# A chain of attention and two mixture layers on one core: the third token chunk's first expert layer rewritten as seven quarter products per pair of feature tiles

## The chip, the core and the metric

One NeuronCore of a Trainium2 chip runs the whole kernel. The metric is the device time of one execution in microseconds, as the median of several runs. The profile is of one execution, taken by the hardware profiler. The engines are called as the profile calls them: PE (TensorE matmul), PEld (its weight loads), DVE (VectorE), ACT (ScalarE), POOL (GpSimd), SP (SyncE, which issues the large transfers).

## What is computed

The reference, cut to what matters (shapes in comments):

```python
x = attention(q, k, v)               # 2 x 8 heads x 768 x 64, window of 128 and 4 sinks
x = x.transpose(...).reshape(1536, 512)
h = x @ w_in                         # 512 x 2048
y = (maximum(h, 0) + alpha * minimum(h, 0)) @ w_out      # 2048 x 512
p = domain_probs / (domain_probs.sum(-1) + 1e-9)         # 1536 x 4
for e in range(4):
    h = maximum(y @ w1[e], 0)        # 512 x 1024, the first expert layer
    out += p[:, e:e+1] * (h @ w2[e]) # 1024 x 512, the second
```

Everything is float32. The change is in the last loop, for the last 512 of the 1536 tokens.

## The kernel before

**Splits.** Each float32 operand of a matmul is held as two parts of type fp32r, a rounded one (names in h: `wh`, `yh`, `th`) and a rest (`wl`, `yl`, `tl`). A product is three matmuls: high by high, high by low, low by high. ACT makes the high part with a copy, POOL or DVE the low part with a subtraction.

**Tiles.** Tokens stand in three chunks of 512 columns (c = 0, 1, 2). `yh[c]`, `yl[c]` hold the first mixture's output, transposed: 128 partitions by four blocks d of 512 tokens. Feature tiles are 128 wide: tiles 0 to 15 belong to the first mixture, 16 to 47 to the experts. A tile's first weights lie in columns 0 to 511 of `wh[k]`, `wl[k]` and its second weights in columns 512 to 1023.

**Stages.** Attention goes on until about 203 us, with the first mixture's first tiles in between. `rest` then runs the first mixture in blocks of tiles (6 to 10, 11 to 15) over the three chunks, and tiles 16 and 17 over the three chunks; in each of its steps the first layer of one tile runs two steps ahead of the second layer of another. `experts` takes tiles 18 to 47 in 15 pairs (k, k+1), one after another.

**One pair** has three parts on PE, in the order written in the program:
- `four(k)`: the first layer of chunks 0 and 1 for both tiles as one 2 by 2 block product in seven block products instead of eight (Winograd's form). Blocks of the activations are halves of d (two of the four blocks) of chunk 0 or 1, 512 columns wide; the sums S2, S3, S4 of such blocks are in `sh`, `sl`, and S1 takes the place of a block of chunk 1. The blocks of the weights are `b11` to `b22` and their differences T, in `th`, `tl`. One block product is 6 matmuls of 512 columns, so 42 in all. Between products ACT copies the first result (`p1`), DVE adds the others up (`u2`, `u3`, `c22`, `c21`, `c12`), ACT writes the rounded ReLU (`relu_hi`, `hh`) and DVE the rest (`relu_lo`, `hl`). The last two `relu_lo` are put off in `self.later` until `leave()`.
- the first layer of chunk 2 by `s1`, tile by tile: 24 matmuls of 512 columns, then `relu`.
- `out(k, c, hid)` for the three chunks: the second layer, 4 blocks of 6 matmuls of 512 columns for each chunk, 72 in all. After each block DVE adds the result, times the share of the expert, to `acc`.

**Weights of later pairs.** `pair` is a generator of eight steps: four splits (ACT, POOL), the differences T (POOL) and two splits of T. `tick()` lets one step of each open generator be issued, `queue` names those that may begin. `load_due` issues the DMAs that refill the four raw buffers (`raws`). `experts` queues the pair after the next one, and ticks once after chunk 2's first layer and after every second block of `out`.

**Buffers.** `wh` and `wl` come from a ring of six buffers each (`EARLY`) in the pool `work`; tiles 6, 7, 14 and 15 have a place of their own in `late[0]`, `late[1]`, and so have `th`, `tl` of the expert pairs, in turn. The pools `late` and `atk` (attention's split operands) are laid out from the top of the memory downwards (`side="right"`). In this layout the two `late` pools begin at byte 221,152 and 212,960 of a partition, both 32 past a multiple of 64; every other tile that PE reads as weights after attention begins at a multiple of 64. PSUM has eight banks, two of each tag (`h`, `o`) in each of two pools (`psum[0]`, `psum[1]`). `out` uses the two `o` banks of `psum[1]`, chunk 2's first layer those of `psum[0]`.

Of the kernel before, what the change touches and what calls it, by code (L numbers as in the profile page):

```python
# [21 lines left out]
P = 128  # L22
# [31 lines left out]
class Body:  # L54
    def __init__(self, ctx, tc, a):
        self.tc, self.nc, self.a = tc, tc.nc, a
        self.base = ctx.enter_context(tc.tile_pool(name="base", bufs=1))
        self.wraw, self.wh, self.wl = {}, {}, {}

        self.raws = [self.base.tile([P, 2 * CH], F32, name=f"wraw{i}") for i in range(RAW)]  # L60
        self.qks = [self.base.tile([P, KW + UN], F32, name=f"qk{i}") for i in range(QK)]
# [227 lines left out]
    def relu_hi(self, h, name):  # L289
        hh = self.wide.tile([P, CH], F32R, tag="gh", name=f"hh{name}", bufs=6)  # L290
        hl = self.wide.tile([P, CH], F32R, tag="gl", name=f"hl{name}", bufs=6)
        self.nc.scalar.activation(hh, h, AF.Relu)
        return hh, hl

    def relu_lo(self, h, parts):
        hh, hl = parts
        self.nc.vector.scalar_tensor_tensor(hl, h, 0.0, hh.bitcast(F32), ALU.max, ALU.subtract)

    def relu(self, h, name):
        parts = self.relu_hi(h, name)  # L300
# [6 lines left out]
    def sums(self):  # L307

        nc, (a, b) = self.nc, (self.acc[0], self.acc[1])

        def split(i, d, x, eng):
            hi, lo = self.sh[i][:, d, :], self.sl[i][:, d, :]
# [4 lines left out]
        t, u = [self.raws[2 + d][:, CH:] for d in range(2)]  # L317
        for d in range(2):
            nc.vector.tensor_tensor(one[d], b[:, d, :], b[:, 2 + d, :], ALU.add)
            nc.vector.tensor_tensor(t, one[d], a[:, d, :], ALU.subtract)  # L320
            split(2, d, t, nc.gpsimd)
            yield
            nc.vector.tensor_tensor(u, a[:, 2 + d, :], t, ALU.subtract)
            split(4, d, u, nc.gpsimd)
            yield
            nc.vector.tensor_tensor(t, a[:, d, :], b[:, d, :], ALU.subtract)
            split(3, d, t, nc.gpsimd)
            yield

        self.sh[1], self.sl[1] = self.xh[1][:, :2, :], self.xl[1][:, :2, :]  # L330
        for d in range(2):
            split(1, d, one[d], nc.vector)
        yield

    def four(self, k):

        nc, mm = self.nc, self.nc.tensor.matmul
        while any(j <= 2 * k for j in self.queue + [j for j, _ in self.flight]):
            self.load_due()
            self.tick()  # L340
        xh, xl, (w, v) = self.xh, self.xl, (k, k + 1)
        low, high = slice(0, UN), slice(UN, CH)
        B = {11: (w, low), 21: (w, high), 12: (v, low), 22: (v, high)}
        B = {i: (self.wh[x][:, c], self.wl[x][:, c]) for i, (x, c) in B.items()}
        T = [(self.th[k][:, i * UN:(i + 1) * UN], self.tl[k][:, i * UN:(i + 1) * UN]) for i in range(4)]
        A = {11: (xh[0][:, :2, :], xl[0][:, :2, :]), 12: (xh[0][:, 2:, :], xl[0][:, 2:, :]),
             22: (xh[1][:, 2:, :], xl[1][:, 2:, :])}
        S = {i: (self.sh[i], self.sl[i]) for i in range(1, 5)}
# [9 lines left out]
        p = [self.psum[i // 2].tile([P, CH], F32, tag="h", name=f"h{k}_{i}", bufs=2) for i in range(4)]  # L358
        p1, u2, u3, c22 = [self.raws[i][:, CH:] for i in range(4)]
        c21, c12 = [self.qks[2 + i][:, :CH] for i in range(2)]  # L360

# [3 lines left out]
        product(p[0], A[11], B[11], True)  # L365
# [7 lines left out]
        h22 = self.relu_hi(c22, f"{k}_22")  # L373
        product(p[0], A[12], B[21], False)
        h11 = self.relu_hi(p[0], f"{k}_11")
        self.relu_lo(c22, h22)
        self.relu_lo(p[0], h11)
        product(p[2], A[22], T[3], False)
        add(c21, p[2], u2)
        h21 = self.relu_hi(c21, f"{k}_21")  # L380
        product(p[3], S[4], B[22], False)
        add(c12, p[3], u2)
        h12 = self.relu_hi(c12, f"{k}_12")
        self.later = [lambda: self.relu_lo(c21, h21), lambda: self.relu_lo(c12, h12)]
        self.hid[k] = [(h11, h12), (h21, h22)]

    def out(self, k, c, hid):

        nc, mm, e = self.nc, self.nc.tensor.matmul, (k - N1) * P // F2
        for d in range(CH // P):  # L390
            ps = self.psum[1].tile([P, CH], F32, tag="o", name=f"o{k}_{c}_{d}", bufs=2)
# [9 lines left out]
            if d % 2:  # L401
                self.load_due()
                self.tick()
# [7 lines left out]
    def experts(self):  # L411
        for k in range(PAIR1, NW, 2):
            if k > PAIR1:
                self.four(k)
            if k + 4 < NW:
                self.queue.append(2 * (k + 4))
            last = []
            for x in range(2):
                ps = self.psum[0].tile([P, CH], F32, tag="o", name=f"h{k}_c{x}", bufs=2)
                self.s1(k + x, self.xh[2], self.xl[2], ps)  # L420
                self.leave()
                last.append(self.relu(ps, f"{k}_c{x}"))
            self.load_due()
            self.tick()
            for c, hid in enumerate(self.hid[k] + [last]):
# [243 lines left out]
    def ahead(self):  # L669
# [6 lines left out]
        self.sh, self.sl, self.th, self.tl, self.hid, self.later = {}, {}, {}, {}, {}, []  # L676
# [113 lines left out]
    def rest(self, pool, units, blk0):  # L790
# [10 lines left out]
        for i in (2, 3, 4):  # L801
            self.sh[i] = pool.tile([P, 2, CH], F32R, name=f"s{i}h")
            self.sl[i] = pool.tile([P, 2, CH], F32R, name=f"s{i}l")
        sums = self.sums()
        with tc.tile_pool(name="psc", bufs=1, space=PSUM) as psc:
            psum = self.psum = [self.psb, psc]
            gs, outs = {}, None
            for i in range(len(steps) + 2):
# [34 lines left out]
                while PAIR1 <= nxt < PAIR1 + 4 and last[nxt + 1 - SLOTS] <= i:  # L843
# [21 lines left out]
                if (k, c) in [(n1 - 1, 2), (n1, 0)]:  # L865
# [151 lines left out]
```

## Time and profile before

| | us |
|---|---|
| median of 3 runs | 906.77 |
| lowest, highest | 905.07, 911.1 |
| profiled execution | 906.78 |
| its span, first to last instruction | 905.0 |

The profiled execution's time is 1.8 us over its span. A busy row of PE counts matmuls that overlap in the pipeline, so distances between starts are read instead. In a timeline row the columns are the start, the duration, the engine, the line, the operation, what it writes from what it reads, the shape, and in brackets the idle time before it with what ended it.

### The profile page before, as it was taken

How to read it: one execution, taken by the hardware profiler on the slowest of the kernel's cores; microseconds unless marked ns; L12 is line 12 of the kernel's file. 1: busy time of each engine (PE TensorE's matmuls, PEld its weight loads, DVE VectorE, ACT ScalarE, POOL GpSimd, SP SyncE). 2: the span in 40 equal slices, each digit the busy share in tenths (PEclk: the TensorE clock that was granted, in tenths of full speed). 3: DMA queues.
4: the chain of work that ended last, by engine and by line, in shares of the span. 5: the costliest groups of instructions: out<-in, count | busy, mean ns of one | idle time of the engine just before them, and what ended most of it. 6: DMA issues, size and time to landing. Idle time of an engine off the chain costs nothing.

```text
span 905.0 us, 12418 instructions
## 1 busy us (share of the span) xinstructions
PE 891.7 (99%) x4670; PEld 739.1 (82%) x4670; DVE 530.0 (59%) x999; ACT 317.2 (35%) x719; POOL 365.0 (40%) x346
## 2 busy tenths in 40 slices
PE   8999999998999999999999999999999999999997
PEld 5678999998888888888888888888888888888886
DVE  6778877648994543545545555455555545555554
ACT  4787766754431222332222231232123113212210
POOL 2456654525672454675415422440442244034000
PEclk9999999999999999999999999999999999999999
DMA  6554432202331020001011101100110111010003
GB/s 184 173 198 145 142 116 93 78 1 95 116 117 47 24 70 1 1 24 47 23 48 47 47 0 47 47 29 18 47 47 1 47 47 38 10 47 1 1 1 144
DMA packets 23718, 54.47 MB, mean 60 GB/s; under 512 B 3168, under 2 KB 3168, under 8 KB 23648
## 3 DMA queue, kind: packets, MB, share of 16 engines
q1 hardware_dynamic: 23504, 53.57, 18.0%
q8 instruction: 39, 0.64, 0.3%
q14 instruction: 31, 0.25, 0.1%
q10 hardware_dynamic: 144, 0.00, 0.0%
HBM read 50.42 MB, written 3.15 MB: 59 GB/s over the span
## 4 chain that ended last, share of the span: by engine, by line
PE 92%; DVE 4%; ACT 1%; issue 1%; POOL 0%; DVEq 0%; ACTq 0%; POOLq 0%
PE o L397 9%; PE o L396 9%; PE o L395 9%; PE h L354 5%; PE h L356 5%; PE h L355 5%; PE h L250 5%; PE h L251 5%; PE h L252 5%; PE o L259 5%; PE o L260 5%; PE o L261 4%; PE h_c L250 3%; PE pv L640 3%; PE h_c L251 3%; PE h_c L252 3%
## 5 line engine op out<-in xcount | busy, mean ns | idle before, releaser
L400 DVE SCALAR_TENSOR_TENSOR acc<-o,prob,acc 128x512 f32<-128x512 f32 x180 | 135.2, 751 | 100.5 <-PE o L397 100.5
L136 POOL TENSOR_TENSOR wl<-wraw,wh 128x512 fp32r<-128x512 f32 x60 | 77.2, 1298 | 273.4 <-ACT wh L135 273.4
L395 PE MATMUL o<-wh,hh 128*128 128x512 f32 x240 | 93.4, 389 | 0.0
L396 PE MATMUL o<-wl,hh 128*128 128x512 f32 x240 | 93.4, 389 | 0.0
L397 PE MATMUL o<-wh,hl 128*128 128x512 f32 x240 | 93.4, 389 | 0.0
L250 PE MATMUL h<-xh,wh 128*128 128x256 f32 (+1 forms) x264 | 90.2, 342 | 0.0
L252 PE MATMUL h<-xh,wl 128*128 128x256 f32 (+1 forms) x264 | 87.7, 332 | 0.0
L251 PE MATMUL h<-xl,wh 128*128 128x256 f32 (+1 forms) x264 | 87.6, 332 | 0.0
L286 POOL TENSOR_TENSOR gl<-qk,gh 128x512 fp32r<-128x512 f32 (+1 forms) x36 | 48.8, 1356 | 72.1 <-ACT gh L285 69.9
L285 ACT ACTIVATE gh<-qk 128x512 fp32r<-128x512 f32 (+1 forms) x36 | 21.5, 598 | 123.9 <-DVE qk L284 121.2
L366 ACT ACTIVATE wraw<-h 128x512 f32<-128x512 f32 x15 | 9.0, 598 | 156.8 <-PE h L356 156.8
L363 DVE TENSOR_TENSOR wraw<-h,wraw 128x512 f32<-128x512 f32 x45 | 31.1, 692 | 51.0 <-PE h L356 49.4
L283 DVE TENSOR_SCALAR qk<-h,alpha 128x512 f32<-128x512 f32 (+1 forms) x36 | 25.3, 704 | 54.6 <-PE h L252 54.5
L260 PE MATMUL o<-gl,wh 128*128 128x512 f32 (+1 forms) x144 | 54.0, 375 | 1.9 <-POOL gl L286 1.9
L250 PEld LDWEIGHTS h<-xh,wh 128*128 128x128 f32 x264 | 49.9, 189 | 6.6 <-issue 1.7
L259 PE MATMUL o<-gh,wh 128*128 128x512 f32 (+1 forms) x144 | 53.8, 374 | 0.5 <-ACT gh L285 0.5
L252 PEld LDWEIGHTS h<-xh,wl 128*128 128x128 f32 x264 | 49.9, 189 | 5.0
L251 PEld LDWEIGHTS h<-xl,wh 128*128 128x128 f32 x264 | 50.0, 189 | 4.9
L261 PE MATMUL o<-gh,wl 128*128 128x512 f32 (+1 forms) x144 | 53.7, 373 | 0.0
L572 ACT ACTIVATE p<-p,nmax 128x288 f32<-128x288 f32 (+1 forms) x96 | 47.8, 500 | 15.9 <-DVE nmax L551 15.8
L396 PEld LDWEIGHTS o<-wl,hh 128*128 128x128 f32 x240 | 45.0, 188 | 9.4
L395 PEld LDWEIGHTS o<-wh,hh 128*128 128x128 f32 x240 | 45.0, 188 | 9.4
(172 smaller groups left out, 2295.8 us busy)
## 6 DMA issues: line engine op xcount, KB each, us to landing
wraw<-in_w SPq DMA_DIRECT2D x32, 512.0 KB, 3.7
wraw<-in_w SPq DMA_DIRECT2D x64, 256.0 KB, 2.9
qk<-in_qk SPq DMA_DIRECT2D x21, 352.0 KB, 3.0
v<-in_v SPq DMA_DIRECT2D x12, 256.0 KB, 3.4
out<-acc SPq DMA_DIRECT2D x12, 256.0 KB, 2.3
qk<-in_qk SPq DMA_DIRECT2D x8, 272.0 KB, 3.2
qk<-in_qk SPq DMA_DIRECT2D x11, 176.0 KB, 3.0
qk<-in_qk SPq DMA_DIRECT2D x8, 136.0 KB, 3.5
```

The costliest lines, as they stand in the source:

```text
L136: nc.gpsimd.tensor_tensor(lo, x, hi.bitcast(F32), ALU.subtract)
L250: mm(ps, wh[:, c], xh[:, dk, :], start=dk == 0, stop=False)
L251: mm(ps, wh[:, c], xl[:, dk, :], start=False, stop=False)
L252: mm(ps, wl[:, c], xh[:, dk, :], start=False, stop=dk == DM // P - 1)
L259: mm(outs[dt], wh[:, c], gh, start=first and begins[dt], stop=False, skip_group_check=True)
L260: mm(outs[dt], wh[:, c], gl, start=False, stop=False, skip_group_check=True)
L261: mm(outs[dt], wl[:, c], gh, start=False, stop=last, skip_group_check=True)
L286: nc.gpsimd.tensor_tensor(gl, g, gh.bitcast(F32), ALU.subtract)
L395: mm(ps, hh[:, n], wh, start=x == 0, stop=False)
L396: mm(ps, hh[:, n], wl, start=False, stop=False)
L397: mm(ps, hl[:, n], wh, start=False, stop=x == 1)
L400: nc.vector.scalar_tensor_tensor(acc, ps, self.prob[:, nt, e:e + 1], acc, ALU.mult, ALU.add)
```

## The change

- `products` is the body of `four`, now with the operands, PSUM tiles, temporaries and results as arguments. `four` calls it as before for chunks 0 and 1.
- `halves(k)` calls it for chunk 2, whose 512 tokens are taken as two halves of 256: seven block products of 6 matmuls of 256 columns, 42 in all. It uses one `o` bank for each of its four PSUM tiles, and 256-column pieces of `qks[:2]`, `warm` and `masks[1]` as temporaries.
- `sums` goes on for three more steps that make S1 to S4 of chunk 2. S2, S3 and S4 lie in `late[0]`, `late[1]`, S1 in the place of a block of chunk 2. `rest` calls it in three more places.
- `th`, `tl` come from the ring `work` like `wh`, `wl`: three of its six buffers for a pair.
- `experts` queues only the next pair, and `out` issues loads and a tick after each block. `out` takes the `o` banks of both PSUM pools in turn. `leave()` is called in `products` after its second product, and after `halves`.
- A tile of 32 bytes a partition is placed at the top, before the `atk` and `late` pools, which lie 32 bytes lower.

```diff
+        top = ctx.enter_context(tc.tile_pool(name="top", bufs=1, side="right"))
+        self.pad = top.tile([P, 8], F32, name="pad")
...
-        late = self.late[k // 2 % 2]
-        th = self.th[k] = late.tile([P, 2 * CH], F32R, tag="wh", name=f"th{k}", bufs=1)
-        tl = self.tl[k] = late.tile([P, 2 * CH], F32R, tag="wl", name=f"tl{k}", bufs=1)
+        th = self.th[k] = self.work.tile([P, 2 * CH], F32R, tag="wh", name=f"th{k}", bufs=EARLY)
+        tl = self.tl[k] = self.work.tile([P, 2 * CH], F32R, tag="wl", name=f"tl{k}", bufs=EARLY)
...
+        a11, a12, a21, a22 = [y[:, d:d + 2, n:n + UN] for n in (0, UN) for d in (0, 2)]
+        late = [[pool.tile([P, 4, UN], F32R, tag=tag, name=f"s2_{tag}", bufs=1) for tag in ("wh", "wl")]
+                for pool in self.late[:2]]
+        self.s2 = {2 + i: [x[:, i % 2 * 2:i % 2 * 2 + 2, :] for x in late[i // 2]] for i in range(3)}
+        self.s2[1] = [x[2][:, :2, UN:] for x in (self.xh, self.xl)]
+        one, t, u = [x.rearrange("p (d n) -> p d n", d=2) for x in (self.qks[0][:, :CH], t, u)]
+        nc.vector.tensor_tensor(one, a21, a22, ALU.add)
+        sub(t, one, a11)
+        split(self.s2[2], t, nc.gpsimd)
+        yield
+        sub(u, a12, t)
+        split(self.s2[4], u, nc.gpsimd)
+        sub(t, a11, a21)
+        split(self.s2[3], t, nc.gpsimd)
+        yield
+        split(self.s2[1], one, nc.vector)
+        yield
...
         product(p[1], S[2], T[1], True)
+        self.leave()
         add(u2, p[1], p1)
...
+    def halves(self, k):
+        xs = (self.xh, self.xl)
+        A = [[x[2][:, d:d + 2, n:n + UN] for x in xs] for n, d in ((0, 0), (0, 2), (UN, 2))]
+        p = [self.psum[i].tile([P, CH], F32, tag="o", name=f"c{k}_{j}", bufs=2)[:, :UN]
+             for j, i in enumerate((0, 1, 0, 1))]
+        temps = [x[:, n:n + UN] for x in self.qks[:2] for n in (0, UN)] + [self.warm, self.masks[1]]
+        h = [self.hidden(f"{k}_c{i}") for i in range(2)]
+        parts = [[x[:, n:n + UN] for x in h[f]] for n in (0, UN) for f in range(2)]
+        self.products(k, A, self.s2, p, temps, parts)
+        self.hid.append(h)
...
-            ps = self.psum[1].tile([P, CH], F32, tag="o", name=f"o{k}_{c}_{d}", bufs=2)
+            ps = self.psum[(d + 1) % 2].tile([P, CH], F32, tag="o", name=f"o{k}_{c}_{d}", bufs=2)
...
-            if d % 2:
-                self.load_due()
-                self.tick()
+            self.load_due()
+            self.tick()
...
-            if k + 4 < NW:
-                self.queue.append(2 * (k + 4))
-            last = []
-            for x in range(2):
-                ps = self.psum[0].tile([P, CH], F32, tag="o", name=f"h{k}_c{x}", bufs=2)
-                self.s1(k + x, self.xh[2], self.xl[2], ps)
-                self.leave()
-                last.append(self.relu(ps, f"{k}_c{x}"))
+            if k + 2 < NW:
+                self.queue.append(2 * (k + 2))
+            self.halves(k)
+            self.leave()
...
-                while PAIR1 <= nxt < PAIR1 + 4 and last[nxt + 1 - SLOTS] <= i:
+                if nxt == PAIR1 and last[nxt + 1 - SLOTS] <= i:
...
-                if (k, c) in [(n1 - 1, 2), (n1, 0)]:
+                if (k, c) in [(n1 - 1, 2), (n1, 0), (n1, 1)] or (k, c, f) == (n1, 2, N1):
                     next(sums)
```

## Rows read from the trace of the kernel before

**Rows 1.** The page: busy time of the engines, and PE's granted clock in slices.

```profile
PE 891.7 (99%) x4670; PEld 739.1 (82%) x4670; DVE 530.0 (59%) x999; ACT 317.2 (35%) x719; POOL 365.0 (40%) x346
PEclk9999999999999999999999999999999999999999
```

**Rows 2.** The page: the chain that ended last, shares of the span by engine.

```profile
PE 92%; DVE 4%; ACT 1%; issue 1%; POOL 0%; DVEq 0%; ACTq 0%; POOLq 0%
```

**Rows 3.** PE's waits: who was waited for, total us, times, longest.

```profile
PE h_c L250 <- DVE acc L863: 0.2, 1, 0.2
```

**Rows 4.** Timeline of PE, one pair: where its three parts and the next pair begin.

```profile
647.39 0.39 PE L354 MATMUL h<-yh,wh 128*128 128x512 f32 x1
...
657.13 0.39 PE L250 MATMUL h_c<-yh,wh 128*128 128x512 f32 x1
...
662.58 0.39 PE L395 MATMUL o<-wh,hh 128*128 128x512 f32 x1
...
678.90 0.39 PE L354 MATMUL h<-yh,wh 128*128 128x512 f32 x1
```

**Rows 5.** Timeline of PE in the same pair: two matmuls three apart on `tl`.

```profile
652.02 0.39 PE L356 MATMUL h<-yh,tl 128*128 128x512 f32 x1
...
652.72 0.40 PE L356 MATMUL h<-yh,tl 128*128 128x512 f32 x1
```

**Rows 6.** Timeline of PE at the end of attention: two runs of 256-column matmuls.

```profile
201.74 0.28 PE L250 MATMUL h<-xh,wh 128*128 128x256 f32 x1
...
203.06 0.28 PE L252 MATMUL h<-xh,wl 128*128 128x256 f32 x1
...
205.33 0.28 PE L259 MATMUL o<-gha,wh 128*128 128x256 f32 x1
...
207.84 0.28 PE L250 MATMUL h<-xh,wh 128*128 128x256 f32 x1
```

**Rows 7.** Timeline of PE in the block of tiles 6 to 10: starts of four steps.

```profile
247.94 0.39 PE L259 MATMUL o<-gh,wh 128*128 128x512 f32 x1
...
250.67 0.39 PE L250 MATMUL h<-xh,wh 128*128 128x512 f32 x1
...
253.46 0.39 PE L259 MATMUL o<-gh,wh 128*128 128x512 f32 x1
...
256.19 0.39 PE L250 MATMUL h<-xh,wh 128*128 128x512 f32 x1
```

**Rows 8.** Timeline of all engines around the end of `four`, same pair.

```profile
649.92 0.40 PE L356 MATMUL h<-s2h,tl 128*128 128x512 f32 x1
650.43 0.69 DVE L363 TENSOR_TENSOR wraw<-h,wraw 128x512 f32<-128x512 f32 x1 [2.09 <-PE h L356]
...
657.33 0.69 DVE L363 TENSOR_TENSOR qk<-h,wraw 128x512 f32<-128x512 f32 x1 [0.70 <-PE h L356]
...
657.94 1.47 DVE L297 SCALAR_TENSOR_TENSOR hl<-qk,hh 128x512 fp32r<-128x512 f32 x2
658.06 0.63 ACT L292 ACTIVATE hh<-qk 128x512 fp32r<-128x512 f32 x1 [0.76 <-DVE qk L363]
```

**Rows 9.** Groups of DVE and ACT by shape: count, then busy us, mean ns.

```profile
L284 DVE SCALAR_TENSOR_TENSOR qk<-h,qk 128x256 f32<-128x256 f32 x6 | 2.5, 424 | 0.2
L320 DVE TENSOR_TENSOR wraw<-wraw,acc 128x512 f32<-128x512 f32 x2 | 2.7, 1351 | 0.1
L326 DVE TENSOR_TENSOR wraw<-acc,acc 128x512 f32<-128x512 f32 x2 | 1.4, 698 | 0.0
L285 ACT ACTIVATE gh<-qk 128x256 fp32r<-128x256 f32 x6 | 2.5, 418 | 12.1 <-DVE qk L284 9.4 <-PE h L252 2.7
```

**Rows 10.** Timeline of POOL: the end of one stretch of `pair` work, and the next stretch.

```profile
641.71 1.29 POOL L136 TENSOR_TENSOR tl<-t,th 128x512 fp32r<-128x512 f32 x1
664.03 1.30 POOL L136 TENSOR_TENSOR wl<-wraw,wh 128x512 fp32r<-128x512 f32 x1 [21.02 <-ACT wh L135]
...
673.18 1.29 POOL L136 TENSOR_TENSOR tl<-t,th 128x512 fp32r<-128x512 f32 x1
```

More of the change, by code (lines that the diff above doesn't have):

```diff
@@ L307, in sums, with sub, split @@
     def sums(self):
-        nc, (a, b) = self.nc, (self.acc[0], self.acc[1])
-        def split(i, d, x, eng):
-            hi, lo = self.sh[i][:, d, :], self.sl[i][:, d, :]
+        nc, (a, b, y) = self.nc, [self.acc[c] for c in range(NC)]
+        def sub(out, a, b):
+            nc.vector.tensor_tensor(out, a, b, ALU.subtract)
+        def split(to, x, eng):
+            hi, lo = to
             nc.scalar.activation(hi, x, AF.Copy)
@@ L317, in sums @@
         t, u = [self.raws[2 + d][:, CH:] for d in range(2)]
+        s = [{i: [x[:, d, :] for x in self.s01[i]] for i in (2, 3, 4)} for d in range(2)]
         for d in range(2):
             nc.vector.tensor_tensor(one[d], b[:, d, :], b[:, 2 + d, :], ALU.add)
[L320 to L321 removed]
+            sub(t, one[d], a[:, d, :])
+            split(s[d][2], t, nc.gpsimd)
             yield
[L323 removed]
@@ L331, in sums @@
         for d in range(2):
-            split(1, d, one[d], nc.vector)
+            split([x[:, d, :] for x in self.s01[1]], one[d], nc.vector)
         yield
-    def four(self, k):
-        nc, mm = self.nc, self.nc.tensor.matmul
-        while any(j <= 2 * k for j in self.queue + [j for j, _ in self.flight]):
-            self.load_due()
-            self.tick()
[L341 to L344, printed above, removed]
+        a11, a12, a21, a22 = [y[:, d:d + 2, n:n + UN] for n in (0, UN) for d in (0, 2)]
@@ L348, in four @@
-        S = {i: (self.sh[i], self.sl[i]) for i in range(1, 5)}
+        b11, b21, b12, b22 = B
+        a11, a12, a22 = A
+        h11, h12, h21, h22 = hid
+        p1, u2, u3, c22, c21, c12 = temps
         def product(ps, a, b, first):
@@ L356, in product @@
                 mm(ps, bl[:, c], ah[:, d, :], start=False, stop=d == 1, skip_group_check=True)
-        p = [self.psum[i // 2].tile([P, CH], F32, tag="h", name=f"h{k}_{i}", bufs=2) for i in range(4)]
-        p1, u2, u3, c22 = [self.raws[i][:, CH:] for i in range(4)]
-        c21, c12 = [self.qks[2 + i][:, :CH] for i in range(2)]
         def add(out, a, b):
             nc.vector.tensor_tensor(out, a, b, ALU.add)
-        product(p[0], A[11], B[11], True)
+        product(p[0], a11, b11, True)
         nc.scalar.activation(p1, p[0], AF.Copy)
         product(p[1], S[2], T[1], True)
+        self.leave()
         add(u2, p[1], p1)
@@ L372, in four @@
         add(c22, p[3], u3)
-        h22 = self.relu_hi(c22, f"{k}_22")
-        product(p[0], A[12], B[21], False)
-        h11 = self.relu_hi(p[0], f"{k}_11")
+        self.relu_hi(c22, h22)
+        product(p[0], a12, b21, False)
+        self.relu_hi(p[0], h11)
         self.relu_lo(c22, h22)
         self.relu_lo(p[0], h11)
-        product(p[2], A[22], T[3], False)
+        product(p[2], a22, T[3], False)
         add(c21, p[2], u2)
-        h21 = self.relu_hi(c21, f"{k}_21")
-        product(p[3], S[4], B[22], False)
+        self.relu_hi(c21, h21)
+        product(p[3], S[4], b22, False)
         add(c12, p[3], u2)
-        h12 = self.relu_hi(c12, f"{k}_12")
+        self.relu_hi(c12, h12)
         self.later = [lambda: self.relu_lo(c21, h21), lambda: self.relu_lo(c12, h12)]
-        self.hid[k] = [(h11, h12), (h21, h22)]
+    def four(self, k):
+        while any(j <= 2 * k for j in self.queue + [j for j, _ in self.flight]):
+            self.load_due()
+            self.tick()
+        xs = (self.xh, self.xl)
+        A = [[x[c][:, d:d + 2, :] for x in xs] for c, d in ((0, 0), (0, 2), (1, 2))]
+        p = [self.psum[i // 2].tile([P, CH], F32, tag="h", name=f"h{k}_{i}", bufs=2) for i in range(4)]
+        temps = [x[:, CH:] for x in self.raws] + [x[:, :CH] for x in self.qks[2:4]]
+        h = [self.hidden(f"{k}_{i}") for i in range(4)]
+        self.products(k, A, self.s01, p, temps, h)
+        self.hid = [h[:2], h[2:]]
+    def halves(self, k):
+        xs = (self.xh, self.xl)
+        A = [[x[2][:, d:d + 2, n:n + UN] for x in xs] for n, d in ((0, 0), (0, 2), (UN, 2))]
[6 more added lines that the diff above has]
+        self.hid.append(h)
     def out(self, k, c, hid):
@@ L801, in rest @@
         for i in (2, 3, 4):
-            self.sh[i] = pool.tile([P, 2, CH], F32R, name=f"s{i}h")
-            self.sl[i] = pool.tile([P, 2, CH], F32R, name=f"s{i}l")
+            self.s01[i] = [pool.tile([P, 2, CH], F32R, name=f"s{i}{x}") for x in "hl"]
         sums = self.sums()
```

36 lines of the change are left out of this document (18 added, 18 removed).

## The prediction

> **What bounds the kernel now.** I read the page first: PE is busy for 99% of the span and its granted clock is at the upper of its two levels, 2.4 GHz, in all 40 slices [rows 1]. The chain of waits says the same from the end backwards: 92% of it is PE [rows 2]. PE's waits show that in the whole expert stage it waited once, 0.2 us, at the first chunk 2 matmul of pair 18 [rows 3]. So from 236 us on nothing but the number of matmuls and the distance from one start to the next sets the time, and only distances are worth reading; all other engines matter only where they could make PE wait. The timeline of one pair gives the distances [rows 4]: `four` takes 657.13 - 647.39 = 9.74 us for 42 matmuls (0.232 each), chunk 2's first layer 662.58 - 657.13 = 5.45 us for 24 (0.227 each), `out` 678.90 - 662.58 = 16.32 us for 72 (0.2267 each), the pair 31.51 us. The other pairs repeat this within 0.01 us, 15 pairs in all.
>
> **The same matmul has two paces.** 512 columns at 2.4 GHz are 213.3 ns; 226.7 is 13.3 more, and 232 is 19 more. The slow pace is that of `four`: two matmuls three apart on `tl` start 0.70 us apart, 0.233 each [rows 5]. What sets it apart is the weight operand: `th`, `tl` lie in the `late` pools, 32 bytes past a multiple of 64, all other weights of this stage at a multiple. The block of tiles 6 to 10 shows it again [rows 7]: the steps that begin at 247.94 and 253.46 are on tiles 8 and 9 and take 2.73 us for 12 matmuls; the one between, 253.46 - 250.67 = 2.79 us, is on tile 6, which lies in `late`. I take the address as the cause; that the `late` pools are also the topmost memory is a rival below.
>
> **Part 1, chunk 2 in quarter products.** Removed on PE: 24 matmuls of 512 columns, 5.44 us a pair. Added: 42 of 256. Their pace is read at the end of attention, where PE runs 256-column matmuls without a break [rows 6]: 1.32 us for 11 distances and 2.51 for 21, so 0.120 both times, again 13.3 ns over the columns (106.7 ns). 42 x 0.120 = 5.04 us. Gain 0.40 us a pair, x 15 = 6.1 us. The ends: the rounding of the rows allows 0.119 to 0.121; the operands of S2 to S4 and the PSUM order are new here, so I widen that to 0.117 and 0.123, a gain of 8.0 or 4.2 us. Equality is at 5.44 / 42 = 0.1296.
> The Trainium skill speaks against this part: TensorE: Matmul & The Clock Gate, "Back-to-back issue gap", gives a sustained spacing, set by matmul and weight load together, of about 81 ns at 128 columns and 131 ns at 512; read in between, an estimate of 98 ns at 256, 42 would cost 4.1 us where 24 cost 3.1, a loss of 15 us in all. The trace doesn't agree: 227 ns at 512 and 120 at 256 [rows 4, 6], and I go by the rows.
>
> **Part 2, T in the ring.** All weights of `four` are then at a multiple of 64, and 42 x 0.2267 = 9.52 us replace 9.74: 0.22 us a pair, 3.3 us in all. The 9.74 is taken whole: it has the products on `wh` in it that stand between those on `th` and are slowed along with them.
>
> **Part 3, the 32-byte tile.** It moves the `late` pools to a multiple of 64. Four tiles (6, 7, 14, 15) are used in three chunks and two layers: 24 steps, each 2.79 - 2.72 = 0.07 us too long, with 0.01 in the step ahead of it [rows 7]: 24 x 0.08 = 1.9 us. Attention's operands move too; they are some 116 matmuls of 288 columns at most, so between nothing and 116 x 6.5 ns = 0.75 us; I take nothing, as no row shows a slow pace at that shape.
>
> **What lies beside PE.** Per pair, DVE gets five adds of 256 columns (0.42 each [rows 9]) and four short ReLU rests for two long ones, 2.4 us more of 31; ACT one copy and four short for two long. What matters is the order in `halves`, with T the start of its first product (657.13 here) and 0.72 us for each product. DVE still has `four`'s last add from T + 0.20 and the two deferred `relu_lo`, which end at T + 2.28 [rows 8]; `leave()` puts them ahead of the first add of `halves`, so they are what the adds queue behind. ACT's last `hh` ends at T + 1.56, `p1` with 0.42 [rows 9] at T + 2.0. Then u2 ends at T + 2.70, u3 at T + 3.12 (its product is there at 17 x 0.12 + 0.51 = T + 2.55, the 0.51 being the lag from the last matmul's start to DVE's [rows 8]), c22 at T + 3.69. PE's sixth product, which needs u3 to have read its bank, starts at T + 3.60, the seventh, behind c22, at T + 4.32. Margins 0.48 and 0.63: no wait, so this costs nothing, but if DVE were half a microsecond later it would. `out` then begins on the bank that u2 has read and has four banks instead of two, so no wait there.
> `pair` work is now done in one go between `halves` and the next `four`. POOL's share of a pair is ten operations, 10.4 us from 664.03 to 674.47 [rows 10]; it can begin about T + 6.9 as now and ends near T + 17.5, while the next `four` needs `th` at its second product, T + 5.04 + 16.32 + 1.36 = T + 22.7. The ring holds: the pair's three buffers of each kind were released with the pair before the last. The loads of one pair's raw tiles are issued during the pair before, on SP, which has nothing else until the last pair's stores; taken as nothing, and 5 us of room cover them.
> The three more steps of `sums` run once, beside the block of tiles 16 and 17: four DVE operations between 0.70 and 1.35 us [rows 9], three splits. They can hold up the first `four` by one such operation at most, between 0 and 1.35 us, once; I take 0, as DVE is busy for 59% of the span [rows 1]. The 0.2 us wait of [rows 3] stays.
>
> **Sum.** 6.1 + 3.3 + 1.9 = 11.3 us off the span of 905.0, which gives 893.7. The profiled execution took 906.78, 1.8 over its span and equal to the median of 906.77; so I forecast 895.4 us, 1.2% less. With the ends above (pace 0.117 to 0.123, attention, `sums`) 893 to 898.
>
> **Rivals.**
> - *A short hand-back wait in `halves`.* The margins of 0.48 and 0.63 are read from a chain of six operations; a lag of 0.1 more at each step of the chain would use them up. A wait of 0.3 us a pair (two thirds of the smaller margin) costs 4.5 us: 899.9. Against it: the same chain in `four` doesn't stop PE once.
> - *The `late` pools are slow because of where they are, not because of the 32 bytes.* Then part 3 gives nothing (1.9 us lost), and 18 of the 42 quarter products' matmuls, which read S2 to S4 from there as the moving operand, could lose the same 6.5 ns: 18 x 6.5 x 15 = 1.8 us. 899.1. For it: before, place and address go together in every slow row, so no row can tell them apart; that the address has the larger part is a judgement.
> - *Half the columns are not half the time.* If what a matmul costs beyond its columns doubled in products with short operands (13.3 to 26.6 ns), 42 x 0.133 = 5.60 us: part 1 loses 0.15 us a pair, 8.3 us behind forecast: 903.7. Against it: the 32 distances of [rows 6].
> - *Slower: DVE and POOL hold each other up at the start of `halves`.* The rows have the same subtraction at 698 and at 1351 ns [rows 9]. If the two deferred `relu_lo`, with two operands in SBUF each, took 1.35 instead of 0.69, u3 would end at T + 4.35 instead of 3.12 and PE would wait 0.75 us, with 0.2 for starting again 0.95 a pair: 14.2 us, 909.6. It decides from a wait of 0.75 us a pair. The Trainium skill has this rule: SBUF — State Buffer, "Who interferes with whom", where a DVE operation with two SBUF inputs and a POOL operation lock each other out; the 1351 ns agree. Against it: it needs POOL at work from T to T + 2.3, and POOL is idle from 643.0 to 664.03, before and after T [rows 10]; the change doesn't bring its next work forward.
> - *That the change is faster than counted:* if short matmuls ran near the bare 106.7 ns, 42 x 13.3 ns x 15 = 8.4 us more: 887.0. No row shows it.
>
> **How the numbers follow.** Forecast 0.68; short wait 0.11; place of the pools 0.10; width 0.04; slower 0.05; much faster 0.02. The likeliest case gives the time, 895.4. The range 892.5 to 901.5 holds the forecast with its ends and the first two rivals, and leaves out the others and their tails, under 2 in 10. A measurement of this kernel can tell about 1% from no change, 897.7 on the one side and 915.8 on the other. Faster by over 1%: the forecast but for its upper tail, the last case, and the weak ends of the first two, 0.70. Within 1%: 0.27, the slower rival's 909.6 with it. Slower by over 1%: 0.03, for that rival with a longer wait.
>
> **What the changed profile would show.** Right: a pair of 30.88 us between the first L-lines of `products`; 42 matmuls of 512 columns in 9.52, 42 of 256 in 5.04, `out` unchanged at 16.32; steps on tiles 6, 7, 14 and 15 at 2.72; no PE wait inside `halves` in the list of waits. Wrong: a distance over 0.25 us at the sixth or seventh quarter product, with DVE as releaser (first rival or, with `relu_lo` at over 1 us, the slower one); steps on tile 6 still at 2.79 and quarter products with S2 to S4 slower than those without (second); an even 0.13 over all 42 (third); PE waiting for POOL at the second product of `four` would mean that `pair` isn't done in time, which I have ruled out by 5 us.

## The result, and the profile after

The changed kernel took 898.83 us (median of four runs, 894.62 to 899.06), the kernel before beside it 906.73 (905.07 to 911.1): a ratio of 0.9889, with an interval of 0.9857 to 0.9922. That is 1.1% faster, inside the range of 892.5 to 901.5, and 3.4 us over the forecast of 895.4. The profiled execution took 898.79 us, its span 897.0, again 1.8 less.

Here "after" is the changed kernel; its lines are L373 to L375 for the products, L435 to L437 for `out`, L298 for `relu_lo`, L378 for the adds, L381 for `p1`, and the results of chunk 2's quarter products are called `c`. The page of after: busy times, PE's clock in slices, and the chain's shares by engine.

```profile
PE 884.5 (99%) x4940; PEld 749.2 (84%) x4940; DVE 561.7 (63%) x1109; ACT 328.9 (37%) x768; POOL 368.9 (41%) x349
PEclk9699999999999999999999999999999999999999
PE 94%; DVE 3%; ACT 1%; issue 1%; POOL 0%; DVEq 0%; ACTq 0%; POOLq 0%
```

Two things differ from [rows 1, 2]: 270 more matmuls (15 pairs by 42 - 24), and a 6 in the second slice of the clock, where before had 9. The first is the change; the second is taken up below.

PE's timeline of the pair that answers to [rows 4]: the starts of `four`, of the quarter products, of `out` and of the next `four`, and between them the first matmul of each quarter product.

```profile
645.17 0.39 PE L373 MATMUL h<-yh,wh 128*128 128x512 f32 x1
...
654.69 0.28 PE L373 MATMUL c<-yh,wh 128*128 128x256 f32 x1
...
655.40 0.29 PE L373 MATMUL c<-s_wh,th 128*128 128x256 f32 x1
...
656.10 0.28 PE L373 MATMUL c<-s_wh,th 128*128 128x256 f32 x1
...
656.78 0.28 PE L373 MATMUL c<-yh,th 128*128 128x256 f32 x1
...
657.49 0.28 PE L373 MATMUL c<-yh,wh 128*128 128x256 f32 x1
...
658.20 0.28 PE L373 MATMUL c<-yh,th 128*128 128x256 f32 x1
...
658.92 0.29 PE L373 MATMUL c<-s_wh,wh 128*128 128x256 f32 x1
...
659.62 0.39 PE L435 MATMUL o<-wh,hgh 128*128 128x512 f32 x1
...
675.95 0.39 PE L373 MATMUL h<-yh,wh 128*128 128x512 f32 x1
```

`four` takes 654.69 - 645.17 = 9.52 us (forecast 9.52), the quarter products 4.93 (5.04), `out` 16.33 (16.32); the pair 30.78 (30.88, and 31.51 before). The quarter products don't all run at one pace. The third, on S3 (`s_wh` is the buffer that holds its high part), takes 656.78 - 656.10 = 0.68 us, 0.113 a matmul; the first six-matmul stretch, on `yh`, and the sixth take 0.71 to 0.72, 0.118 to 0.120. From the first `four` to the last matmul of the span it is 478.3 us before and 467.4 after: 10.9 us less.

DVE, ACT and POOL beside it (start, duration; "x3" is three in a row; in brackets idle time and who ended it). They answer to [rows 8, 10].

```profile
654.89 0.69 DVE L378 TENSOR_TENSOR qk<-h,wraw 128x512 f32<-128x512 f32 x1 [0.67 <-PE h L375]
655.50 1.48 DVE L298 SCALAR_TENSOR_TENSOR hgl<-qk,hgh 128x512 fp32r<-128x512 f32 x2
656.89 1.47 DVE L378 TENSOR_TENSOR qk<-c,qk 128x256 f32<-128x256 f32 x3
...
656.15 0.36 ACT L381 ACTIVATE qk<-c 128x256 f32<-128x256 f32 x1
...
638.53 2.53 POOL L139 TENSOR_TENSOR tl<-t,th 128x512 fp32r<-128x512 f32 x2
661.38 2.57 POOL L139 TENSOR_TENSOR wl<-wraw,wh 128x512 fp32r<-128x512 f32 x2 [20.32 <-ACT wh L138]
...
669.32 2.54 POOL L139 TENSOR_TENSOR tl<-t,th 128x512 fp32r<-128x512 f32 x2
```

With T = 654.69, the two deferred `relu_lo` run from T + 0.81 to T + 2.29 (forecast: to T + 2.28), the three adds end at T + 3.67 (forecast for c22: 3.69), POOL idles for 20.32 us across T and ends the next pair's work at T + 17.2 (17.5). PE's waits (who was waited for, total us, times, longest):

```profile
PE o L262 <- POOL gl L288: 2.5, 3, 0.9
...
PE s L568 <- DVE nmax L586: 1.0, 1, 1.0
...
PE c L373 <- DVE acc L897: 0.2, 1, 0.2
```

There is none inside the quarter products; the 0.2 us of [rows 3] stayed.

So the expert stage gave more than forecast, and yet the kernel is later than forecast. The difference arises before the expert stage: the first `four` starts at 423.79 us, 2.9 us later than before (420.90), though part 3 should have brought it forward. The table of windows (busy time by engine, then the granted clock, 1.00 for 2.4 GHz and 0.50 for 1.2) shows where. After:

```profile
20.00:25.00 5.00, 3.94 (x14) 2.21 (x15) 2.89 (x12) 3.34 (x11) 2.22 (x2) 0.66 0.53 162
25.00:30.00 5.00, 5.00 (x18) 2.82 (x15) 3.47 (x12) 0.42 (x1) 1.72 (x3) 0.50 0.76 228
30.00:35.00 5.00, 5.00 (x16) 2.78 (x16) 1.31 (x5) 2.84 (x10) 1.44 (x2) 0.50 0.68 210
35.00:40.00 5.00, 5.00 (x24) 3.28 (x20) 3.25 (x11) 2.20 (x7) 0.73 (x1) 0.63 0.36 127
```

The same stretch before:

```profile
20.00:25.00 5.00, 3.79 (x15) 1.89 (x15) 3.65 (x14) 2.97 (x10) 1.55 (x3) 0.82 0.48 155
25.00:30.00 5.00, 4.63 (x24) 2.93 (x21) 3.62 (x13) 1.58 (x6) 2.22 (x3) 0.84 0.84 255
30.00:35.00 5.00, 4.50 (x27) 2.60 (x26) 3.54 (x15) 3.51 (x14) 2.44 (x3) 1.00 0.95 267
```

A mean of 0.66 over 5 us is (1 - 0.66) / 0.5 x 5 = 3.4 us at the lower level. Summed up, after ran 3.4 + 5 + 5 + 3.7 = 17.1 us of attention at 1.2 GHz, before 1.8 + 1.6 = 3.4. PE did the same ahead of it in both: it waited 1.0 us for the DVE operation that makes `nmax` out of earlier scores (the wait on `nmax` above; PE's timelines of after, then of before):

```profile
21.62 1.65 PE L568 MATMUL s<-qk 64*128 64x128 f32 x4 [1.00 <-DVE nmax L586]
```

```profile
22.37 1.16 PE L533 MATMUL s<-qk 64*128 64x128 f32 x4 [1.00 <-DVE nmax L551]
```

The theory that I took to the chip: the pair became 0.72 us shorter for the reasons forecast, the weights' address sets the pace of part 2 and 3, and the length of the low-clock stretch has nothing to do with the change. The rivals: the topmost place sets the pace (the prediction's second rival); quarter products gain only because the moving operand or some address is good, not by their columns; the change itself prolongs the low stretch.

### The profile page after: what moved, and what is told of

It reads as the page before. It is cut to its first block, busy times and chain, and to the rows that moved or that the text cites. A ratio compares the mean times of both kernels' runs of the same rounds, so it can differ in the third digit from the quotient of the medians.

```text
span 897.0 us, 13164 instructions
## 1 busy us (share of the span) xinstructions
PE 884.5 (99%) x4940; PEld 749.2 (84%) x4940; DVE 561.7 (63%) x1109; ACT 328.9 (37%) x768; POOL 368.9 (41%) x349
## 4 chain that ended last, share of the span: by engine, by line
PE 94%; DVE 3%; ACT 1%; issue 1%; POOL 0%; DVEq 0%; ACTq 0%; POOLq 0%
PE o L436 9%; PE o L437 9%; PE o L435 9%; PE h L373 5%; PE h L375 5%; PE h L252 5%; PE h L374 5%; PE h L253 5%; PE h L254 5%; PE o L261 5%; PE o L262 5%; PE o L263 5%; PE pv L675 3%; PE c L373 3%; PE c L375 3%; PE c L374 3%
## 5 line engine op out<-in xcount | busy, mean ns | idle before, releaser
L436 PE MATMUL o<-wl,hgh 128*128 128x512 f32 x240 | 93.6, 390 | 0.0
L437 PE MATMUL o<-wh,hgl 128*128 128x512 f32 x240 | 93.5, 390 | 0.0
L435 PE MATMUL o<-wh,hgh 128*128 128x512 f32 x240 | 93.5, 390 | 0.0
L252 PE MATMUL h<-xh,wh 128*128 128x256 f32 (+1 forms) x264 | 90.2, 342 | 0.0
L378 DVE TENSOR_TENSOR wraw<-h,wraw 128x512 f32<-128x512 f32 x45 | 31.1, 692 | 48.2 <-PE h L375 46.3
L381 ACT ACTIVATE wraw<-h 128x512 f32<-128x512 f32 x15 | 8.9, 596 | 140.9 <-PE h L375 140.9
L252 PEld LDWEIGHTS h<-xh,wh 128*128 128x128 f32 x264 | 50.0, 189 | 6.5 <-issue 1.7
L437 PEld LDWEIGHTS o<-wh,hgl 128*128 128x128 f32 x240 | 45.1, 188 | 9.4
L435 PEld LDWEIGHTS o<-wh,hgh 128*128 128x128 f32 x240 | 45.1, 188 | 8.8
```

Source lines behind the costliest of these rows:

```text
L252: mm(ps, wh[:, c], xh[:, dk, :], start=dk == 0, stop=False)
L435: mm(ps, hh[:, n], wh, start=x == 0, stop=False)
L436: mm(ps, hh[:, n], wl, start=False, stop=False)
L437: mm(ps, hl[:, n], wh, start=False, stop=x == 1)
```

## The experiments

A name with a_ is an edit of the changed kernel, one with b_ an edit of the kernel before. Times are medians; the ratio is to the kernel before, run beside it. The granted clock is that of the whole span, and it tells the length of the low stretch: 0.997 or more for at most a few us of it, about 0.99 for a long one (13.7 us in the profiled a_again and a_yshift, 17.1 in after, b_pad32, a_pad96 and a_mixed). Since either can occur in one and the same kernel, the runs of before fall into two groups, 905.0 to 907.1 and 910.7 to 911.8 us, and so do those of after, 892.9 to 895.4 and 898.7 to 899.5; medians are compared only at like clock.

### The tile's size: address or place?

Five runs put the `late` pools at other addresses. Before without a tile has them at 224 past a multiple of 256, and the change at 192.

```diff
+        top = ctx.enter_context(tc.tile_pool(name="top", bufs=1, side="right"))
+        self.pad = top.tile([P, 8], F32, name="pad")     # b_pad32: before with the tile
+        self.pad = top.tile([P, 16], F32, name="pad")    # b_pad64: before, 64 bytes
-        self.pad = top.tile([P, 8], F32, name="pad")     # a_nopad: after without the tile
+        self.pad = top.tile([P, 24], F32, name="pad")    # a_pad96: after, 96 bytes
+        self.pad = top.tile([P, 56], F32, name="pad")    # a_pad224: after, 224 bytes
```

a_pad224 also has the two fillers (idle matmuls) of a_before, told further down, and is compared with a_before. The expectations, in the order of the diff:

> The kernel before with the 32-byte tile alone. If the address sets the pace of the late weights: th products and steps on tiles 6, 7, 14, 15 go from 0.233 us a matmul to the 0.229 that the changed kernel shows on tile 6, so four takes 9.6 us for 9.74 and a step on tile 6 2.75 for 2.79, some 3 us in all off 906.8. If the place at the top of the memory sets it: 0.233 and 2.79 stay, 906.8. The stretch of low clock near 22 us after the start may be short or long in either.

> The kernel before with a tile of 64 bytes: the late pools move further down than with 32, but their address is again 32 past a multiple of 64. Address: 0.233 us a matmul on th and 2.79 us a step on tile 6, as before. Place: whatever 32 bytes lower gave, 64 gives too.

> The changed kernel without the 32-byte tile. Forecast's part 3: steps on tile 6 back at 2.79 us, 1 to 2 us more in all. The quarter products whose moving operand S2 to S4 lies in late run at 0.113 us in the changed kernel, those on yh at 0.120. If that comes from where late lies: 0.113 again, 4.93 us for 42. If from its address: another pace, 0.120 or over, 5.04 us or more.

> The changed kernel with a tile of 96 bytes: the late pools begin at a multiple of 128. If the weights' price goes by the distance from a multiple of 128: steps on tile 6 at 2.72 us instead of 2.75. If the moving operand is fast because it starts 64 past a multiple of 128 while the weights start at a multiple: S2 to S4 products slow down from 0.113 to 0.120, 42 in 5.04 us. If it is the place: 0.113 stays, 4.93.

> The kernel a_before with the late pools at 0 modulo 256 instead of 192 (a tile of 224 bytes instead of 32). Address: steps on tile 6 fall from 2.747 to 2.72 us, the rest of part 3, 0.6 us in all; the quarter products on S2 to S4 rise from 0.113 to about 0.120, 42 in 5.04 us for 4.93, 1.6 us in all; so 1 us slower than a_before's 894.2. Place: tile 6 stays at 2.747, though the pools are still the topmost.

Measured:

| run | `late` mod 256 | step on tile 6, us | 512 columns on T in `late`, ns | quarter products, us | time, us | ratio |
|---|---|---|---|---|---|---|
| before | 224 | 2.791 | 233.4 | - | 906.73 | - |
| b_pad32 | 192 | 2.747 | 229.0 | - | 907.46 (clock 0.99) | 0.9958 [0.9941, 0.9974] |
| b_pad64 | 160 | 2.798 | 233.3 | - | 905.57 (one run, clock 0.999) | |
| after | 192 | 2.748 | - | 4.932 | 898.83 | 0.9889 [0.9857, 0.9922] |
| a_nopad | 224 | 2.792 | - | 4.996 | 896.29 (clock 0.99 to 0.999) | 0.9854 [0.9821, 0.9887] |
| a_pad96 | 128 | 2.795 | - | 4.998 | 901.9 (clock 0.99) | 0.9896 [0.9879, 0.9912] |
| a_pad224 | 0 | 2.720 | - | 5.032 | 895.15 (clock 0.998) | 0.9843 [0.9808, 0.9878] |

PE's timeline, one step on tile 6 and the step behind it, in after, b_pad64 and a_pad224 (the answer to [rows 7]):

```profile
254.61 0.39 PE L252 MATMUL h<-xh,wh 128*128 128x512 f32 x1
...
257.36 0.39 PE L261 MATMUL o<-gh,wh 128*128 128x512 f32 x1
...
260.08 0.39 PE L252 MATMUL h<-xh,wh 128*128 128x512 f32 x1
```

```profile
248.91 0.39 PE L253 MATMUL h<-xh,wh 128*128 128x512 f32 x1
...
251.70 0.40 PE L262 MATMUL o<-gh,wh 128*128 128x512 f32 x1
```

```profile
250.05 0.39 PE L253 MATMUL h<-xh,wh 128*128 128x512 f32 x1
...
252.77 0.39 PE L262 MATMUL o<-gh,wh 128*128 128x512 f32 x1
...
255.49 0.39 PE L253 MATMUL h<-xh,wh 128*128 128x512 f32 x1
```

2.75 us in after, 2.79 in b_pad64, 2.72 in a_pad224. In all seven kernels the pools are the topmost but for the tile, and the pace goes with the address: the rival of place falls. But "a multiple of 64" falls too: 128 is one, and is as slow as 224 and 160 (the expectation for a_pad96 had 2.72, in case a multiple of 128 was enough); 192 gives most of the gain; with the moving operand at 0, as here, only 0 gives all. b_pad32 also prices the address alone: at like clock (0.99) 907.5 against 911.3 for the kernel before, 4 us. In b_pad64 two other steps, on tiles 9 and 10 whose weights lie at a multiple of 256, were slower as well (2.77 and 2.76 against 2.73 and 2.72 before). They are the steps that follow directly on a step on tile 6 or 7, and with `late` at 128 (a_pad96) the same two take 2.76 and 2.75. So a slow step seems to slow the step behind it, more at 160 and 128 than at 224; that this is the cause was not tried.

The quarter products go the other way. The matmuls that read S2 to S4 from `late` as the moving operand were on average 115.5 ns apart at 192 (113.3 in the third product), 118.2 at 224 (short of the 120 that was expected for another address), 118.9 at 128 and 120.0 at 0; those on `yh`, at a multiple of 256, took 118.9 to 119.7 on average in each of these runs. So the address that is best for weights is the slowest for the moving operand of 256 columns: a_pad224 has 24 steps that are 0.028 us shorter, 0.7 us, and gives 15 x 0.10 = 1.5 back; its median is 0.9 us over that of a_before. Without the tile (a_nopad) the change is 2.9 us slower at like clock, 901.7 against 898.8.

### The moving operand alone: a_yshift

`xh`, `xl`, `yh`, `yl` moved to 192 past a multiple of 256.

```diff
     def new_x(self, c, name="x"):
+        if "low" not in vars(self):
+            self.low = self.work.tile([P, 48], F32, name=f"low{name}")
...
+        if "high" not in vars(self):
+            self.high = self.work.tile([P, 16], F32, name=f"high{name}")
```

> The changed kernel with xh, xl, yh, yl moved up by 192 bytes, to an address of 192 modulo 256, where S2 to S4 of the quarter products lie in the changed kernel; weights stay at 0 modulo 256. If a moving operand at 192 modulo 256 is read faster (0.113 instead of 0.120 us at 256 columns): the quarter products take 4.75 us, and if the 7 ns hold at 512 columns as well, first layers and four go from 0.2267 to 0.220, some 4 us in the expert stage and 1 in the mixture before. If the pace of S2 to S4 was theirs alone: 4.93 and 0.2267.

Measured: 903.29 us, ratio 0.9934 [0.9909, 0.9959]; at a clock near 0.99 that is 4.5 us slower than after. `four` went from 9.52 to 9.72 us, 233.3 ns for each matmul of 512 columns on `yh`, with weights at a multiple of 256; the quarter products stayed at 4.947, an even 117.8 ns. Neither branch of the expectation came out, and the guess that a moving operand at 192 is faster is wrong as a rule: with weights at a multiple of 256 it costs 6.6 ns at 512 columns and gains about 2 at 256.

The same trace has the case in which both operands lie at 192: the first layer of tiles 6, 7, 14 and 15, whose weights are in `late`. PE's timeline, a step on tile 6, the step behind it, and the same for tile 8, whose weights are at a multiple of 256:

```profile
253.59 0.39 PE L252 MATMUL h<-xh,wh 128*128 128x512 f32 x1
...
256.32 0.39 PE L261 MATMUL o<-gh,wh 128*128 128x512 f32 x1
...
264.57 0.39 PE L252 MATMUL h<-xh,wh 128*128 128x512 f32 x1
...
267.38 0.40 PE L261 MATMUL o<-gh,wh 128*128 128x512 f32 x1
```

By these rows tile 6 takes 2.73 us and tile 8 2.81. With both operands at 192, 512 columns run at 227.7 ns, 1.0 over the 226.7 with both at 0, while either operand alone at 192 costs 2.3 (weights) or 6.6 (moving operand). So it is not that each operand wants a multiple of 256; of the pairs that were run the two with equal offsets are the fast ones, and no other equal pair was tried. Nor do a matmul's own two addresses give its pace alone. The third quarter product reads S3 at 192, with weights at a multiple of 256, in both kernels; it runs at 113.3 ns in after and at 117.8 here, where of the operands of PE only `xh`, `xl`, `yh` and `yl` have changed their offset.

### Columns or addresses: a_mixed

In every pair with k a multiple of 4 (7 of 15) chunk 2 is computed by 24 matmuls of 512 columns, as in the kernel before. S1 has taken the place of a block of chunk 2 by then, so these pairs compute something else.

```diff
-            self.halves(k)
+            if k % 4:
+                self.halves(k)
+            else:
+                last = []
+                for x in range(2):
+                    ps = self.psum[0].tile([P, CH], F32, tag="o", name=f"h{k}_c{x}", bufs=2)
+                    self.s1(k + x, self.xh[2], self.xl[2], ps)
...
```

> The changed kernel with chunk 2's first layer by full matmuls (24 of 512 columns) in the pairs whose k is a multiple of 4, by quarter products in the others. If part 1's gain is the matmuls' own distances: 5.44 us in the one kind of pair, 4.93 in the other, everything else in a pair alike (four 9.52, out 16.32), so 30.79 and 31.28 us a pair. If the quarter products push work elsewhere that costs PE time later in the pair: out or the next four is longer after quarter products by part of the 0.5 us.

Measured: 903.41 us (one run, clock 0.99). One of these pairs on PE's timeline (lines as in after, L252 is `s1`):

```profile
647.75 0.39 PE L373 MATMUL h<-yh,wh 128*128 128x512 f32 x1
...
657.27 0.39 PE L252 MATMUL h_c<-yh,wh 128*128 128x512 f32 x1
...
662.71 0.39 PE L435 MATMUL o<-wh,hgh 128*128 128x512 f32 x1
...
679.03 0.39 PE L373 MATMUL h<-yh,wh 128*128 128x512 f32 x1
```

5.44 us for the 24, `out` 16.32, the pair 31.28, with the same buffers and the same `four`; the pairs between have 4.932, 16.335 and 30.787. So part 1 alone is worth 0.508 - 0.015 = 0.49 us a pair, and it comes from the distances of its own matmuls. The rival that only a good address makes them cheap falls with a_pad224: with all operands at a multiple of 256 the 42 take 5.03 us, still 0.41 less than the 24, so about 0.10 of the 0.51 is the address of S2 to S4.

### The margin: a_dve

0, 1, 2 or 3 idle additions of 256 columns on DVE ahead of u2, by turns.

```diff
         self.leave()
+        for i in range(k // 2 % 4 if temps[4] is self.warm else 0):
+            add(self.scratch, p[1], p1)
         add(u2, p[1], p1)
```

> The changed kernel with 0, 1, 2 or 3 extra adds of 256 columns (about 0.42 us each on DVE) ahead of u2 in the quarter products, by pair: k/2 modulo 4. Nothing else reads what they write. If the margin at the sixth quarter product is the 0.4 to 0.5 us that the chain gives: 4.93 us for the 42 matmuls with none, the same or up to 0.1 more with one, 0.3 to 0.5 more with two, 0.7 to 1.0 more with three, and the waiting matmul is the first of the sixth product. If DVE is far from the bound (rival): 4.93 in all four. If a short wait is there already: each extra add costs 0.42 from the first.

Measured: 900.02 us (one run, clock 0.998). The quarter products took 4.93 us with none, 5.04 with one, 5.50 to 5.67 with two, 5.96 with three. PE's timeline at the sixth product of a pair with three, and the waits of PE in the whole run:

```profile
499.21 0.28 PE L376 MATMUL c<-yh,wl 128*128 128x256 f32 x1
500.26 0.39 PE L374 MATMUL c<-yh,th 128*128 128x256 f32 x1 [0.78 <-DVE qk L379]
500.49 0.28 PE L375 MATMUL c<-yl,th 128*128 128x256 f32 x1
```

```profile
PE c L374 <- DVE qk L379: 4.4, 8, 0.8
```

It is the first matmul of the sixth product that waits, the one whose bank u3 must have read, as the prediction had it. Its start moves from 120 ns behind the matmul before to about 140, 600 and 1060 with one, two and three (with one it stays at 120 in the first pair): 0.46 us for each addition beyond the first, and 0.02 for the first. The margin is thus 0.46 - 0.02 = 0.44 us, where 0.48 was forecast. A wait also makes the next distance 223 instead of 120 ns, 0.10 us for starting again (0.2 was assumed).

### The low-clock stretch: a_before, b_before, a_again

One idle `busy` matmul (two instructions of 256 columns in the trace) ahead of the scores of two heads, in after and in before; and after once more, unchanged.

```diff
+BEFORE = (6, 8)
...
+                if p in BEFORE:
+                    self.busy(psb, 1, f"before{p}", tag="h", bufs=2)
                 for j in [0, 1] if p == 0 else [p + 1] if p + 1 < SOON else [] if p < SOON else [p]:
                     self.at_scores(j)
```

> The changed kernel with one more filler matmul (0.7 us) ahead of the scores of two heads, where PE waits 1 us for DVE at about 20.5 and 27 us and the clock falls in most runs. If that pause is what lets the clock fall to 1.2 GHz and the long stretch costs 4.3 us: granted clock 0.997 to 0.999 in most runs, 892 to 895 us. If the fall has another cause: as often as in the changed kernel (3 of 4 runs at 0.99), 898.8, or more by what the fillers hold up.

> The kernel before with the same two filler matmuls as a_before. If the scatter of both kernels is the stretch of low clock and the change doesn't touch it: granted clock 0.999 and 905.0 to 906.0 us in nearly all runs, instead of 906.7 or 911.3; and a_before's 894.2 below that by 11 to 12 us, which is the change by itself. If the fillers help only the changed kernel's attention: 911 stays the commonest time.

> The changed kernel once more. If the low clock comes by chance in both kernels: two groups of times, near 894.6 and near 898.8, the second the larger. If something in the change brings it: 898.8 in all runs, while the kernel before beside it has both of its groups.

Measured: a_before 894.24 us (893.53 to 894.65, six runs, clock 0.998 or 0.999 in each), ratio 0.9845 [0.9818, 0.9871]; b_before 906.27 (905.43 to 906.72, twelve runs, clock 0.998 to 1.0), ratio 0.997 [0.9952, 0.9988]; a_again 897.01 (892.88 to 899.54), three of its six runs at a clock of 0.99 and three at 0.997 or more. The timeline of PE in a_before, at the place where after and before waited 1.0 us:

```profile
20.91 0.60 PE L236 MATMUL before<-warm 128*128 128x256 f32 x2
22.07 1.04 PE L569 MATMUL s<-qk 64*128 64x128 f32 x4 [0.56 <-DVE nmax L587]
```

And its windows:

```profile
20.00:25.00 5.00, 4.29 (x25) 2.51 (x25) 3.69 (x14) 3.27 (x11) 1.72 (x2) 1.00 0.56 167
25.00:30.00 5.00, 4.38 (x19) 2.58 (x19) 4.90 (x16) 2.26 (x9) 2.38 (x3) 1.00 0.89 236
```

The pause before the scores is 0.56 us instead of 1.00 and the clock stays at 2.4 GHz. The low stretch is gone in the profiled execution of both kernels with fillers, a granted clock of 0.998 or more leaves no room for a long one in any of their runs, and each has one group of times instead of two. That the change prolongs the stretch is refuted: it was long in 6 of 10 executions of after and in 26 of 44 of before, whose runs beside a_before had a median of 910.7. (For a_again the second group was expected to be the larger; it was half.)

The pause by itself does not bring the fall. a_nopad, without fillers, waited 1.0 us for `nmax` even twice, and its clock stayed at 2.4 GHz; here are the first of the two pauses, and its windows:

```profile
21.44 1.04 PE L566 MATMUL s<-qk 64*128 64x128 f32 x4 [1.00 <-DVE nmax L584]
```

```profile
20.00:25.00 5.00, 4.00 (x23) 2.46 (x24) 3.67 (x14) 3.69 (x12) 2.35 (x3) 1.00 0.66 195
25.00:30.00 5.00, 3.95 (x18) 2.07 (x18) 4.40 (x15) 2.37 (x9) 2.09 (x3) 1.00 0.92 248
```

The profiled b_pad64 and a_dve show the same. The fillers both shorten the pause and give PE more matmuls there, and no run separates the two. Nor are they free: in a_dve, with no filler and no low stretch, the first `four` starts at 418.11 us, in a_before at 418.74. This fits the miss in b_before, expected at 905.0 to 906.0 us: ten of its twelve runs were above, while before without fillers took 905.0 to 905.2 in the executions with a clock of 0.999.

The two kernels with fillers give the price of the change without the low stretch: 906.27 - 894.24 = 12.0 us, a ratio of 0.987. They ran on two chips, but the kernel before, run beside each, had the same median on both, 910.7. a_before is the fastest kernel measured here by its median, 1.5% under before.

## Why the prediction was right, and where its sizes were off

**What bounds the kernel.** Right: PE's distances set the time from the first `four` to the end, and no other engine's added work made PE wait.

**Part 1** was forecast at 6.1 us and gave 7.5: 14 pairs at 5.444 - 4.932 = 0.512, the first pair at 5.615 - 5.039 = 0.576, less 15 x 0.015 for a slightly longer `out`. (The first pair, which starts behind the wait of [rows 3], is slower than the others in both kernels, so the pairs of before were not all within 0.01 us of each other.) The mechanism (256 columns cost half of 512 within 5% on average, 42 short for 24 long) held, a_mixed shows it; the term was mis-sized mainly because the matmuls on S2 to S4 run at 115.5 ns on average and not at the 120 of [rows 6]. It is inside the ends of 4.2 and 8.0 that were given.

The Trainium skill (TensorE: Matmul & The Clock Gate, "Back-to-back issue gap") spoke against this part with a sustained spacing of about 131 ns at 512 columns. The trace doesn't agree for these matmuls: it has 226.7 ns at 512 columns and 117.4 on average at 256, so that the 42 are cheaper than the 24, where the estimate from the Trainium skill's figures made them dearer.

**Part 2** was forecast at 3.3 us and gave 15 x (9.742 - 9.520) = 3.3.

**Part 3** was forecast at 1.9 us; the steps went from 2.791 to 2.748, and 24 x (0.043, and 0.01 in the step ahead) = 1.3; with fillers in both kernels the first `four` starts 420.20 - 418.74 = 1.5 us earlier. The step that failed is "32 bytes past a multiple of 64" as what makes the slow pace. The address is the cause, as taken; but 192 past a multiple of 256 is still 2 ns a matmul slower than 0, 128 is no better than 224, and by a_yshift the address of the other operand counts too.

**What was costed at nothing.** The chain in the quarter products came out within 0.02 us of forecast at `relu_lo` and c22, and the margin was 0.44 us for 0.48. POOL was done 5 us ahead of need. The three more steps of `sums` left no wait of their own; the waits on POOL's `gl` add up to 2.5 us in three against 1.9 in before, which may be the clock's doing, as a_before has 1.9.

**The sum.** 7.5 + 3.3 + 1.3 = 12.1, against a forecast of 11.3; the two kernels with fillers show 12.0 by their medians and 904.2 - 891.9 = 12.3 by the spans of their profiled executions. The term that was missing is the clock: the sum was made against an execution with 3.4 us at 1.2 GHz, and the profiled one of after had 17.1. From after to a_before the first `four` moves from 423.79 to 418.74, 5.0 us; from before to b_before from 420.90 to 420.20, 0.7. The difference, 4.3 us, takes 906.8 - 12.3 = 894.5 to the 898.8 that was profiled. The prediction took [rows 1] for a clock of 2.4 GHz throughout. That row did show a 9 in every slice of the clock; a slice of 22 us with 3.4 at half speed is 0.92, so that row could not show it, and the windows of 5 us could.

That the range held is in part luck. The time lies outside the 893 to 898 that the forecast's own ends gave, and inside the stated range only by the room left for two rivals that did not occur. Which stretch each median got was chance as well: long in three of after's four executions and in one of before's four, beside the 6 of 10 and 26 of 44 over all runs. With a short stretch in after's median the time would have been near 895, the forecast.

**The rivals.** No hand-back wait (none in the list, a margin of 0.44). Not the place. Not the width: 0.117 and not 0.133. The lock of DVE and POOL did not come about: the two deferred `relu_lo` took 1.48 us together, and POOL was idle for 20.32 us across them; the condition that the prediction named for it was not met, and no run here created it, so what the lock would cost in this place was not tried. Much faster: part of it is real, 113 ns in one product, where this rival took 106.7 for all.

What stays open: why the address matters as it does (weights of 512-column matmuls, with the moving operand at 0: 226.7 ns at 0, 229 at 192, 233 at 128, 160 and 224 past a multiple of 256), why equal offsets of 192 are nearly as fast as two at 0, why the moving operand's best address differs with the number of columns and with the matmuls around it, and what decides in one execution between no stretch, a short and a long one at the lower clock.

## What to carry to other kernels

Where PE never waits, read the distance between starts for each shape and each pair of operands, and let a term of the sum rest on the same shape at the same address; here the sum then came within 1.0 us of the 12.3 that the change gained. Compare the granted clock in fine windows before comparing times: a stretch of 17 us at half clock early in the span hid a third of what this change gained. Where the end of a pause stands in the list of waits and the clock falls behind it, one idle matmul put into the pause is a cheap trial; here two of them took the median of after from 898.8 to 894.2 us, more than part 2 or part 3 of the change gave.

## What the runs showed of the hardware that was not expected

The same fp32r matmul of 512 columns takes 226.7, 229 or 233 ns by the start address of its weights alone (a_pad224, b_pad32, b_pad64), and 233.3 by that of its moving operand alone (a_yshift); with both at 192 past a multiple of 256 it takes 227.7 (a_yshift). At 256 columns S2 to S4 took 120.0 ns at 0 (a_pad224) and 115.5 at 192 (after), but 117.8 at 192 when all the other moving operands lay at 192 too (a_yshift): the matmuls around it count as well.

Executions of one and the same kernel fall, by chance, into two groups of times 4 to 6 us apart; in the profiled ones PE had none or 3.4 us of attention at 1.2 GHz, or 13.7 to 17.1. A pause of 1.0 us stood ahead of the fall, but a_nopad, b_pad64 and a_dve had the pause without the fall. None of the 22 executions with the fillers (a_before, b_before, a_pad224), which cut the pause to 0.56 us, had the long stretch.
